# A short convolution moved from 64x64 to 32x32 tiles of the array, in a fused attention and gated-unit kernel

## The chip, the cores and the metric

The kernel runs on one core of one Trainium2 chip. Its time is the device time of one execution in microseconds (us). TensorE multiplies matrices, VectorE (DVE) and ScalarE (ACT) read its results in PSUM and work on them, GpSimd (POOL) converts types and writes masks in SBUF, SyncE (SP) issues nearly all DMAs. Lower is better.

## The reference

The first part is attention over 8 batches of 8 heads, 576 positions and 64 features, causal by blocks of 64 positions. Its output, with the 512 features of a position side by side, is the input `x` of a gated unit:

```python
for k in range(K):                                   # K = 5 taps
    gate_pre += conv_w[k][None, None, :] * xp[:, k:k + S, :]
gate = 1.0 / (1.0 + np.exp(-gate_pre))
val = x @ w_val
return (gate * val @ w_out).astype(np.float32)
```

The convolution works on each feature by itself: five taps along the sequence, padded with four zeros ahead of it. The kernel computes in fp16 with fp32 sums.

## The kernel before

**Attention by pairs of heads.** The loop runs over steps `p`; step p handles one of 32 pairs of heads (four pairs are a batch). The order of the work is written out by hand, and every engine takes its instructions in that order. In the middle of the program one step issues on TensorE, in this order: two score tiles of pair p (`s_tile(p, 0)` and `s_tile(p, 1)`), the product of probabilities and values of pair p-1 (`av`, 30 matmuls in two groups, one for each head), the transposes of q and k of pair p+2 (`trans`, and once a batch `trans_tails`), the third score tile (`s_tile(p, 2)`), one unit of the convolution (`conv`), once a batch `s_last`, the transposes of the finished attention (`xtrans`), one tile of the output projection (`out_tile`), and one chunk of the value projection (`val`).

**Who reads what.** ACT applies exp to each score tile (128x1024 elements) and tanh to the convolution, since a sigmoid is (1 + tanh(z/2))/2, and copies the output tiles. DVE normalises the attention (`rc`, then `x`, for each head), copies the transposed q and k (`qkT`) and x (`xt`), and multiplies gate and value (`gv`). POOL casts q, k and v to fp16 and zeroes the masked probabilities.

**PSUM.** Score tiles have a pool of their own with two buffers of two banks each (`psS`). Everything else takes one of four banks in turn (`gbank`, the tiles G): `av` takes two, `trans`, `trans_tails`, `xtrans` and `out_tile` one each, `conv` two, `val` two. So whoever takes a bank waits until the reader of the bank's last content, four takings earlier, has finished.

**The convolution as matmuls.** Features lie on the partitions in four chunks g of 128. A tap is a matmul with a diagonal block of weights (`DG`) against x shifted by the tap, and five taps add up in PSUM. A 64x64 block uses a quarter of the array, so four such matmuls with different quarters are in work at once: a unit `conv(b, c2, hf)` is half the chunks and half a batch (288 positions), 5 x 4 = 20 matmuls. It puts the features into PSUM in another order, and the columns of `w_val` and the rows of `w_out` are permuted to match when they are loaded and cast (`load_w_out`, `weights`).

**Lags and the end.** Convolution runs at step p for unit p-3, `val` for chunk p-4 of both halves of a batch, and a pair of batches gives nine output tiles. After the last pair of heads, five more steps finish what lags. SP issues the loads of step p (`loads(p)`: q and k of pair p+4, v of pair p+2, weights in the first steps), and after the first output tile its stores stand in the same queue.

Of the kernel before, what the change touches and what calls it, by code (L numbers as in the profile page):

```python
# [10 lines left out]
def kernel(  # L11
# [10 lines left out]
    nc = tc.nc  # L22
# [27 lines left out]
    idfold = const([128, 1, 64], fp16, "idfold")  # L50
# [6 lines left out]
    DG = const([128, 20, 64], fp16, "DG")  # L57

    NV, NPT, NX = 4, 3, 3
    v16s = [const([128, 4, 2, 65], fp16, f"v16_{i}") for i in range(NV)]  # L60
# [10 lines left out]
    def gbank():  # L71
        ring[0] += 1
        return GT[(ring[0] - 1) % 4]
# [171 lines left out]

    th = {}

    def conv(b, c2, hf):
        t = th.get((b, c2))
        if t is None:  # L250
            t = th[(b, c2)] = p3.tile([128, 2, 2, 288], fp32, tag="th", name="th")
        rr = (gbank(), gbank())
        for kk in range(5):
            for row, col in ((0, 0), (1, 1), (0, 1), (1, 0)):
                g = 2 * c2 + col
                rs, cs = slice(64 * row, 64 * row + 64), slice(64 * col, 64 * col + 64)
                mm(rr[row][cs, 0:288], DG[rs, 5 * g + kk, 0:64],
                   xts[b % NX][rs, g, kk + 288 * hf:kk + 288 * hf + 288],
                   start=(kk == 0), stop=(kk == 4))
        for row in range(2):  # L260
            nc.scalar.activation(out=t[0:128, row, hf, 0:288], in_=rr[row][0:128, 0:288],  # L261
                                 func=AF.Tanh, bias=0.0, scale=0.5)

    def val(b, x):
        c2, row = divmod(x, 2)
# [3 lines left out]
        t = th[(b, c2)]  # L269
        for hf in range(2):  # L270
            r = gbank()
            for fc in range(4):
                mm(r[0:128, 0:288], w_val_sb[0:128, fc, 128 * x:128 * x + 128],
                   xts[b % NX][0:128, fc, 4 + 288 * hf:4 + 288 * hf + 288],
                   start=(fc == 0), stop=(fc == 3))
            nc.vector.scalar_tensor_tensor(  # L276
                out=gv[u][0:128, x, bi, hf, 0:288], in0=t[0:128, row, hf, 0:288], scalar=1.0,
                in1=r[0:128, 0:288], op0=ALU.add, op1=ALU.mult)
        if row == 1:
            th.pop((b, c2))  # L280

    def out_tile(u, t):
        g = gv[u][0:128].rearrange("p g b f s -> p g (b f s)")
        r = gbank()
        for fc in range(4):
            mm(r[0:128, 0:512], g[:, fc, 128 * t:128 * t + 128],
               w_out_sb[0:128, fc, 0:512], start=(fc == 0), stop=(fc == 3))
        o = p4.tile([128, 512], fp32, tag="osb", name="osb")
        if u == B // 2 - 1 and t >= 4 and t % 2 == 0:
            nc.vector.tensor_copy(out=o[0:128], in_=r[0:128, 0:512])  # L290
# [16 lines left out]
    for hh in range(2):  # L307
        hs = slice(64 * hh, 64 * hh + 64)
        nc.vector.tensor_copy(out=idfold[hs, 0, 0:64], in_=ident16[hs, 64 * hh:64 * hh + 64])
    load_qk1(1)  # L310
    load_v1(0)
    load_vtail(0)
# [43 lines left out]
        nc.sync.dma_start(out=w_st[0:128, 2 * f:2 * f + 2],  # L356
                          in_=moe_w_val[256 * f:256 * f + 256].rearrange("(f p) n -> p f n", p=128))

    def load_w_out(col):
        for x in range(2):  # L360
            nc.sync.dma_start(
                out=w_st2[64 * col:64 * col + 64].rearrange("p (a x) n -> p a x n", a=2)[:, :, x],
                in_=moe_w_out.rearrange("(a c x i) n -> c x i a n", a=2, c=2, x=2)[col, x])

    def weights(s):
        if s == 1:
            nc.vector.tensor_tensor(out=DG[0:128], in0=idfold[0:128].to_broadcast([128, 20, 64]),
                                    in1=convT[0:128].to_broadcast([128, 20, 64]), op=ALU.mult)
        if 3 < s < 8:
            x = s - 4  # L370
            nc.vector.tensor_scalar(
                out=w_val_sb[0:128, 0:4, 128 * x:128 * x + 128].rearrange(
                    "p f (c i) -> p f c i", c=2),
                in0=w_st[0:128].rearrange("p f (a c r i) -> p f a r c i",
                                          a=2, c=2, r=2)[:, :, x // 2, x % 2],
                scalar1=0.5, scalar2=None, op0=ALU.mult)
        if s in (7, 8):
            a = 2 * (s - 7)
# [19 lines left out]
    for p in range(NP + 5):  # L398
        if p < NP:
            loads(p)  # L400
            if p > 0:
                s_tile(p, 0)
                s_tile(p, 1)
        weights(p)
        if 0 <= p - 1 < NP:
# [5 lines left out]
        if 0 < p < NP:  # L411
# [19 lines left out]
        if 0 <= p - 1 < NP:  # L431
            xtrans(p - 1)

        if p >= 8 and p % 4 == 0:
            b = p // 4 - 2
            outs += [(b // 2, t) for t in (range(4) if b % 2 == 0 else range(4, 9))]
        n = 2 if len(outs) == 5 or p == NP + 4 else 1
        for _ in range(n):
            if outs:
                out_tile(*outs.pop(0))  # L440
        if 0 <= p - 4 < NP:
            val(*divmod(p - 4, 4))
    while outs:
        out_tile(*outs.pop(0))


# [28 lines left out]
```

## Time and profile before

| | |
|---|---|
| time, median of 3 runs | 211.24 us (210.98 to 214.17) |
| the profiled execution's own time | 210.69 us |
| its span, first to last instruction | 208.6 us |
| TensorE busy | 191.0 us, 92% |
| DVE, ACT, POOL busy | 131.0, 140.0, 82.9 us |
| moved by DMA | 40.34 MB, 193 GB/s on the mean |
| mean granted TensorE clock | 0.983 |

In rows of the timeline the first number is the start in us from the beginning of the span, the second the duration, then the engine, the line of the kernel, the operation, the tiles (out<-in), the shape, and xN for N instructions merged; in brackets stands how long the engine sat idle and what ended that. In the chain of waits (the work that ended last, followed back) a row is start, duration and what held the end at that time. In grouped rows the numbers behind the bar are busy us, mean ns of one, and idle us before. A matmul's modelled end includes its way through the array, so the distance between starts is what a stream of them costs.

### The profile page before, as it was taken

To read this page: it belongs to the slowest core of one execution; us is meant where nothing else is said; L and a number is where in the kernel's file an instruction comes from. 1 tells how busy PE (TensorE), PEld (TensorE's weight loads), DVE (VectorE), ACT (ScalarE), POOL (GpSimd) and SP (SyncE) were. 2 spreads that over 40 slices of the span, in tenths; PEclk is the share of its full clock that TensorE was granted. 3 is DMA by queue.
4 is the path that set the end of the run, shared out by engine and by line. 5 is a ranking of instruction groups with operands and counts; after the bars stand their busy time and mean duration, and the time that the engine had idled before them with its cause. 6 is when DMAs were issued, how large, how long until landed. Compare 5 with 4: busy or idle time off the path is not lost.

```text
span 208.6 us, 7431 instructions
## 1 busy us (share of the span) xinstructions
PE 191.0 (92%) x3041; PEld 130.5 (63%) x3041; DVE 131.0 (63%) x282; ACT 140.0 (67%) x205; POOL 82.9 (40%) x168
## 2 busy tenths in 40 slices
PE   4699889988999999999999999999999999999992
PEld 1377656665666766676666766676666766666550
DVE  3349878876667657666667657666667657555351
ACT  4347877657776877668776877668776877783421
POOL 6364654566454441445454441445454441120000
PEclk9958999999999999999999999999999999999999
DMA  5999999999777687765776688665866635111235
GB/s 155 271 262 300 300 262 239 214 208 235 177 199 189 192 236 227 220 186 147 229 206 186 197 231 260 189 184 151 241 197 181 201 101 154 53 50 55 101 141 215
DMA packets 70220, 40.34 MB, mean 193 GB/s; under 512 B 48165, under 2 KB 64549, under 8 KB 70186
## 3 DMA queue, kind: packets, MB, share of 16 engines
q1 hardware_dynamic: 69904, 39.60, 70.6%
q8 instruction: 24, 0.39, 0.8%
q10 hardware_dynamic: 282, 0.27, 0.4%
q14 instruction: 10, 0.08, 0.2%
HBM read 30.42 MB, written 9.44 MB: 191 GB/s over the span
## 4 chain that ended last, share of the span: by engine, by line
PE 53%; DVE 19%; DMA 16%; SPq 6%; issue 3%; POOL 2%; DVEq 0%; POOLq 0%
PE G L33 41%; DVE qkT L162 9%; PE S L33 8%; DVE x L232 6%; DMA vs<-in_v_dram 4%; DMA w_st<-in_moe_w_out_dram 4%; DVE rc L231 3%; SPq L83 3%; DMA tlst<-in_k_dram 3%; PE G L241 3%; DMA vtst<-in_v_dram 3%; SPq L103 2%; DMA qks<-in_k_dram 2%; PE G L151 1%; POOL qk L126 1%
## 5 line engine op out<-in xcount | busy, mean ns | idle before, releaser
L185 ACT ACTIVATE pt<-S 128x1024 f16<-128x1024 f32 x96 | 94.3, 1023 | 32.4 <-PE S L33 31.0
L276 DVE SCALAR_TENSOR_TENSOR gv<-th,G 128x288 f16<-128x288 f32 x64 | 29.1, 455 | 37.1 <-PE G L33 34.8
L201 POOL MEMSET pt<- 64x384 f16 x32 | 13.2, 413 | 93.8 <-ACT pt L185 93.8
L162 DVE COPY qkT<-G 128x1024 f16<-128x1024 f16 x31 | 37.7, 1217 | 2.9 <-PE G L151 2.7
L33 PE MATMUL G<-w_out,gv 128*128 128x512 f16 x144 | 35.8, 378 | 2.5 <-DVE qkT L162 2.5
L33 PE MATMUL G<-xt,w_val 128*128 128x288 f16 x256 | 36.8, 286 | 0.4 <-DVE qkT L162 0.3
L33 PEld LDWEIGHTS <-pt 128*128 128x128 f16 x960 | 31.5, 98 | 7.0 <-issue 6.1
L33 PE MATMUL G<-v,pt 128*128 128x65 f16 x896 | 34.3, 195 | 0.1
L126 POOL CAST qk<-qks 128x1024 f16<-128x1024 f32 x31 | 32.6, 1053 | 4.3 <-DMA qks<-in_k_dram 3.6
L232 DVE TENSOR_TENSOR x<-G,rc 128x320 f16<-128x320 f32 x64 | 31.5, 492 | 2.3 <-DVE rc L231 0.2
L292 ACT COPY osb<-G 128x512 f32<-128x512 f32 x33 | 19.3, 586 | 20.1 <-PE G L33 17.9
L33 PEld LDWEIGHTS <-w_val 128*128 128x128 f16 x256 | 25.0, 98 | 12.1 <-issue 0.7
L33 PE MATMUL S<-qkT 64*128 64x512 f16 (+1 forms) x248 | 28.2, 305 | 0.4 <-ACT pt L195 0.4
L33 PE MATMUL G<-xt,DG 64*64 64x288 f16 x640 | 26.3, 287 | 0.0
L261 ACT ACTIVATE th<-G 128x288 f32<-128x288 f32 x64 | 22.7, 412 | 4.8 <-PE G L33 4.8
L33 PEld LDWEIGHTS <-qkT 64*128 64x128 f16 x496 | 15.1, 95 | 14.6 <-issue 7.3
L33 PEld LDWEIGHTS <-gv 128*128 128x128 f16 x144 | 13.7, 97 | 15.1 <-issue 4.2
L151 PE MATMUL G<-ident,qk 128*128 128x128 f16 x256 | 20.6, 225 | 2.8 <-POOL qk L126 2.7
L231 DVE RECIPROCAL rc<-G 128x5 f32<-128x5 f32 x64 | 12.1, 189 | 15.5 <-PE G L33 15.4
L131 POOL CAST v<-vs 128x512 f16<-128x512 f32 x32 | 20.1, 627 | 3.5 <-PE S L33 1.5
L151 PEld LDWEIGHTS <-qk 128*128 128x128 f16 x256 | 15.6, 101 | 4.1 <-POOL qk L126 3.4
L33 PEld LDWEIGHTS <-DG 64*64 64x64 f16 x640 | 16.2, 105 | 2.7 <-issue 0.5
(51 smaller groups left out, 122.5 us busy)
## 6 DMA issues: line engine op xcount, KB each, us to landing
out_dram<-osb SPq DMA_DIRECT2D x36, 256.0 KB, 2.1
qks<-in_q_dram SPq DMA_DIRECT2D x32, 256.0 KB, 3.7
vs<-in_v_dram SPq DMA_DIRECT2D x64, 128.0 KB, 4.3
qks<-in_k_dram SPq DMA_DIRECT2D x31, 256.0 KB, 3.9
tlst<-in_q_dram SPq DMA_DIRECT2D x8, 128.0 KB, 4.2
tlst<-in_k_dram SPq DMA_DIRECT2D x8, 128.0 KB, 4.2
vtst<-in_v_dram SPq DMA_DIRECT2D x8, 128.0 KB, 4.9
w_st<-in_moe_w_val_dram SPq DMA_DIRECT2D x2, 512.0 KB, 6.1
```

What stands on the lines that cost most here:

```text
L33: nc.tensor.matmul(out=out, lhsT=lhsT, rhs=rhs, start=start, stop=stop, skip_group_check=True)
L126: nc.gpsimd.tensor_copy(out=o, in_=s)
L131: nc.gpsimd.tensor_copy(out=v16s[p % NV][0:128, 0:4, 0:2, 0:64], in_=s)
L151: nc.tensor.transpose(out=r[:, o:o + 128], in_=t[0:128, c, 2 * i:2 * i + 2, 0:64], identity=ident16[0:128, 0:128])
L162: nc.vector.tensor_copy(out=o[0:128].rearrange("p i (s n) -> p i s n", n=4), in_=src)
L185: nc.scalar.activation(out=pts[p % NPT][0:128, 0:2, 512 * t:512 * t + 512], in_=s[0:128, 0:2, 0:512], func=AF.Exp, bias=0.0, scale=0.125)
L201: nc.gpsimd.memset(pt[64:128, 0:2, 0:1536].rearrange("p h (t s) -> p h t s", t=3)[:, :, :, 0:64], 0.0)
L231: nc.vector.reciprocal(out=rc[0:128], in_=O[:, :, 64:65])
L232: nc.vector.tensor_tensor(out=x[0:128, 0:5, h, 0:64], in0=O[:, :, 0:64], in1=rc[0:128].to_broadcast([128, 5, 64]), op=ALU.mult)
L261: nc.scalar.activation(out=t[0:128, row, hf, 0:288], in_=rr[row][0:128, 0:288], func=AF.Tanh, bias=0.0, scale=0.5)
L276: nc.vector.scalar_tensor_tensor(out=gv[u][0:128, x, bi, hf, 0:288], in0=t[0:128, row, hf, 0:288], scalar=1.0, in1=r[0:128, 0:288], op0=AL ...
L292: nc.scalar.copy(out=o[0:128], in_=r[0:128, 0:512])
```

## The change

The convolution's blocks become 32x32, sixteen of them in work at once. A unit is now `conv(b, hf)`: all four chunks of half a batch, 5 x 16 = 80 matmuls of the same 288 columns. Row strip `row` of every chunk goes to a bank of its own; two of the four banks come from the score pool `psS`, two from `gbank`. ACT applies tanh to the two score banks in one instruction and to the other two in one each.

A unit runs every other step (odd p, from 5 on), and `val(b, hf, x)` handles one half batch and one chunk, two a step. Output tiles are freed by half batches (`complete`), and the first comes at step 7 where it came at step 8. The loop ends with the last pair of heads; what remains is written out behind it. The permutation of the weights is by 32 features; `w_out` is loaded in steps 3 and 4 (four DMAs to 32 partitions) where it was in steps 4 and 5 (four to 64 partitions), and cast at steps 6 and 7 where it was at 7 and 8.

```diff
-    def conv(b, c2, hf):
...
-        rr = (gbank(), gbank())
-        for kk in range(5):
-            for row, col in ((0, 0), (1, 1), (0, 1), (1, 0)):
-                g = 2 * c2 + col
-                rs, cs = slice(64 * row, 64 * row + 64), slice(64 * col, 64 * col + 64)
-                mm(rr[row][cs, 0:288], DG[rs, 5 * g + kk, 0:64],
...
+    def conv(b, hf):
+        t = th[(b, hf)] = p2.tile([128, 4, 288], fp32, tag="th", name="th")
+        s = psS.tile([128, 2, 512], fp32, tag="S", name="S")
+        ga, gb = gbank(), gbank()
+        rr = (s[0:128, 0], s[0:128, 1], ga[0:128], gb[0:128])
         for kk in range(5):
+            for d in range(4):
+                for row in range(4):
+                    g = (row + d) % 4
+                    rs, cs = slice(32 * row, 32 * row + 32), slice(32 * g, 32 * g + 32)
+                    mm(rr[row][cs, 0:288], DG[rs, 5 * g + kk, 0:32],
+                       xts[b % NX][rs, g, kk + 288 * hf:kk + 288 * hf + 288],
+                       start=(kk == 0), stop=(kk == 4))
+        nc.scalar.activation(out=t[0:128, 0:2, 0:288], in_=s[0:128, 0:2, 0:288],
+                             func=AF.Tanh, bias=0.0, scale=0.5)
+        for row in (2, 3):
+            nc.scalar.activation(out=t[0:128, row, 0:288], in_=rr[row][:, 0:288],
                                  func=AF.Tanh, bias=0.0, scale=0.5)
...
-        if u == B // 2 - 1 and t >= 4 and t % 2 == 0:
+        if u == B // 2 - 1 and t >= 6 and t % 2 == 0:
             nc.vector.tensor_copy(out=o[0:128], in_=r[0:128, 0:512])
...
-    def load_w_out(col):
...
+    def load_w_out(j):
+        nc.sync.dma_start(
+            out=w_st2[32 * j:32 * j + 32],
+            in_=moe_w_out[128 * j:128 * j + 128].rearrange("(x a) n -> a x n", x=4))
...
-        if p in (4, 5):
-            load_w_out(p - 4)
+        if p in (3, 4):
+            load_w_out(2 * p - 6)
+            load_w_out(2 * p - 5)
...
+    def complete(b, hf):
+        n = 2 * (b % 2) + hf
+        outs.extend((b // 2, t) for t in range(2 * n, 9 if n == 3 else 2 * n + 2))
...
-        if 0 <= p - 3 < NP:
-            bq, un = divmod(p - 3, 4)
-            conv(bq, un // 2, un % 2)
+        bq, m = divmod(p - 5, 4)
+        if bq >= 0 and m % 2 == 0:
+            conv(bq, m // 2)
         if p % 4 == 3 and p + 1 < NP:
             s_last((p + 1) // 4)
...
+        out()
+        if len(outs) > 2:
+            out()
+        if bq >= 0:
+            for x in (0, 1):
+                val(bq, m // 2, 2 * (m % 2) + x)
+            if m % 2 == 1:
+                complete(bq, m // 2)
...
+    b = B - 1
+    av(NP - 1)
+    out()
+    for x in (2, 3):
+        val(b - 1, 1, x)
+    complete(b - 1, 1)
+    xtrans(NP - 1)
+    out()
+    conv(b, 0)
+    out()
+    conv(b, 1)
+    out()
+    for hf in range(2):
+        for x in range(4):
+            val(b, hf, x)
+            out()
+        complete(b, hf)
     while outs:
-        out_tile(*outs.pop(0))
+        out()
```

First place: TensorE in one step in the middle of the program, before the change. One matmul of each group is shown; S_ are score tiles, G0 to G3 the four banks, ident16 marks a transpose.

```order
L33 MATMUL G3_106<-v16t_0_89,pt4_0_96 128x65
...
L151 MATMUL G0_103<-ident16_76,qk16_2217 128x128
...
L33 MATMUL S_2327<-kt_0_98,qkT_2060 128x64
...
L33 MATMUL G1_104<-xt_0_100,DG_84 64x288
...
L241 MATMUL G3_106<-ident16_76,x16_2280 128x128
...
L33 MATMUL G0_103<-w_out_79,gv_1729 128x512
...
L33 MATMUL G1_104<-xt_0_100,w_val_78 128x288
...
L33 MATMUL G2_105<-xt_0_100,w_val_78 128x288
```

The same engine with the change, in step 20, one of the steps that have no convolution.

```order
L33 MATMUL G2_105<-v16t_1_90,pt4_1_97 128x65
...
L151 MATMUL G3_106<-ident16_76,qk16_2225 128x128
...
L33 MATMUL S_2411<-kt_0_98,qkT_2099 128x64
...
L241 MATMUL G0_103<-ident16_76,x16_2364 128x128
...
L33 MATMUL G1_104<-w_out_79,gv_2026 128x512
...
L33 MATMUL G2_105<-xt_2_102,w_val_78 128x288
...
L33 MATMUL G3_106<-xt_2_102,w_val_78 128x288
```

Before, the output tile takes the bank that the transposes of q and k used in the same step (G0); now it takes the first bank of `av` (G1), and the second chunk of `val` takes the transposes' bank (G3).

Second place: ACT over one step with the convolution and `s_last`, before. pt is exp's output, th tanh's, osb an output tile.

```order
L185 ACTIVATE pt_0_93<-S_2062 128x2x512
L261 ACTIVATE th_2080<-G3_106 128x288
L261 ACTIVATE th_2080<-G0_103 128x288
L195 ACTIVATE pt4_0_96<-S_2103 128x512
L292 COPY osb_2123<-G2_105 128x512
```

With the change, step 19:

```order
L185 ACTIVATE pt_0_93<-S_2209 128x2x512
L261 ACTIVATE th_2227<-S_2228 128x576
L264 ACTIVATE th_2227<-G3_106 128x288
L264 ACTIVATE th_2227<-G0_103 128x288
L195 ACTIVATE pt4_0_96<-S_2312 128x512
L291 COPY osb_2332<-G2_105 128x512
```

The convolution's score buffer S_2228 comes between S_2209 (the third score tile) and S_2312 (`s_last`), so with two buffers `s_last` now writes the one that exp of the third score tile reads; before, S_2103 had the other.

Third place: SP's queue around the loads of `w_out`, before.

```order
L103 DMA vs_456<-in_v_dram 128x4x64 x2
L92 DMA tlst<-in_q_dram 64x8x64
L92 DMA tlst<-in_k_dram 64x8x64
L83 DMA qks_576<-in_q_dram 128x2x256
L83 DMA qks_576<-in_k_dram 128x2x256
L103 DMA vs_579<-in_v_dram 128x4x64 x2
L361 DMA w_st_81<-in_moe_w_out_dram 64x2x512 x2
L83 DMA qks_698<-in_q_dram 128x2x256
L83 DMA qks_698<-in_k_dram 128x2x256
L103 DMA vs_701<-in_v_dram 128x4x64 x2
L361 DMA w_st_81<-in_moe_w_out_dram 64x2x512 x2
```

With the change:

```order
L103 DMA vs_458<-in_v_dram 128x4x64 x2
L359 DMA w_st_81<-in_moe_w_out_dram 32x4x512 x2
L92 DMA tlst<-in_q_dram 64x8x64
L92 DMA tlst<-in_k_dram 64x8x64
L83 DMA qks_557<-in_q_dram 128x2x256
L83 DMA qks_557<-in_k_dram 128x2x256
L103 DMA vs_560<-in_v_dram 128x4x64 x2
L359 DMA w_st_81<-in_moe_w_out_dram 32x4x512 x2
L83 DMA qks_646<-in_q_dram 128x2x256
L83 DMA qks_646<-in_k_dram 128x2x256
L103 DMA vs_649<-in_v_dram 128x4x64 x2
```

Each pair of `w_out` loads now stands ahead of the q, k and v of one more step: v of pair 6 (vs_579 before, vs_560 now) comes behind one pair of them where it came behind none, and v of pair 7 behind both where it came behind one.

More of the change, by code (lines that the diff above doesn't have):

```diff
@@ L56 @@
     convT = const([128, 20, 1], fp16, "convT")
[L57 removed]
+    DG = const([128, 20, 32], fp16, "DG")
     NV, NPT, NX = 4, 3, 3
@@ L246, with val @@
     th = {}
[L248 to L261 removed]
+    def conv(b, hf):
[3 more added lines that the diff above has]
+        rr = (s[0:128, 0], s[0:128, 1], ga[0:128], gb[0:128])
+        for kk in range(5):
+            for d in range(4):
[9 more added lines that the diff above has]
+            nc.scalar.activation(out=t[0:128, row, 0:288], in_=rr[row][:, 0:288],
                                  func=AF.Tanh, bias=0.0, scale=0.5)
[L264 to L265 removed]
+    def val(b, hf, x):
         u, bi = divmod(b, 2)
@@ L268, in val @@
             gv[u] = p2.tile([128, 4, 2, 2, 288], fp16, tag="gv", name="gv")
[L269 to L280, printed above, removed]
+        t = th[(b, hf)]
+        r = gbank()
+        for fc in range(4):
+            mm(r[0:128, 0:288], w_val_sb[0:128, fc, 128 * x:128 * x + 128],
+               xts[b % NX][0:128, fc, 4 + 288 * hf:4 + 288 * hf + 288],
+               start=(fc == 0), stop=(fc == 3))
+        nc.vector.scalar_tensor_tensor(
+            out=gv[u][0:128, x, bi, hf, 0:288], in0=t[0:128, x, 0:288], scalar=1.0,
+            in1=r[0:128, 0:288], op0=ALU.add, op1=ALU.mult)
     def out_tile(u, t):
@@ L306 @@
         nc.vector.memset(ktails[i][0:128, 0:4, 1:2, 64:128], 0.0)
-    for hh in range(2):
-        hs = slice(64 * hh, 64 * hh + 64)
-        nc.vector.tensor_copy(out=idfold[hs, 0, 0:64], in_=ident16[hs, 64 * hh:64 * hh + 64])
+    for i in range(4):
+        hs = slice(32 * i, 32 * i + 32)
+        nc.vector.tensor_copy(out=idfold[hs, 0, 0:32], in_=ident16[hs, 32 * i:32 * i + 32])
     load_qk1(1)
@@ L393, in loads, with out @@
             load_w_val(p - 1)
-        if p in (4, 5):
-            load_w_out(p - 4)
+        if p in (3, 4):
+            load_w_out(2 * p - 6)
+            load_w_out(2 * p - 5)
     outs = []
[L398 to L403, printed above, removed]
+    def complete(b, hf):
+        n = 2 * (b % 2) + hf
+        outs.extend((b // 2, t) for t in range(2 * n, 9 if n == 3 else 2 * n + 2))
+    def out():
+        if outs:
+            out_tile(*outs.pop(0))
+    for p in range(NP):
+        loads(p)
+        if p > 0:
+            s_tile(p, 0)
+            s_tile(p, 1)
         weights(p)
-        if 0 <= p - 1 < NP:
+        if p > 0:
             av(p - 1)
@@ L410 @@
                 trans_tails((p + 2) // 4)
-        if 0 < p < NP:
+        if p > 0:
             s_tile(p, 2)
```

33 lines of the change are left out of this document (9 added, 24 removed).

## The prediction

> **What bounds the kernel now.** I read the page, then the chain of waits, then the timeline of one step. The page's busy times and its chain by engine:
>
> ```profile
> PE 191.0 (92%) x3041; PEld 130.5 (63%) x3041; DVE 131.0 (63%) x282; ACT 140.0 (67%) x205; POOL 82.9 (40%) x168
> PE 53%; DVE 19%; DMA 16%; SPq 6%; issue 3%; POOL 2%; DVEq 0%; POOLq 0%
> ```
>
> TensorE is busy 92%, yet only 53% of the chain: a fifth goes through DVE. Where, the chain shows for step 17, the pattern of the whole middle:
>
> ```profile
> 100.38 2.00 PE G L33 x12
> 102.38 0.54 PE S L33 x6
> 102.92 0.57 PE G L33 x15
> 103.75 0.26 DVE x L232
> 104.37 0.49 DVE x L232
> 104.86 1.14 DVE qkT L162
> ```
>
> From the first head's product the end is held by DVE: normalise twice, then copy qkT until 106.0. TensorE's timeline, steps 17 to 19:
>
> ```profile
> 102.31 0.61 PE L33 MATMUL S<-qkT 64*128 64x512 f16 x6
> 102.85 0.60 PE L33 MATMUL G<-v,pt 128*128 128x65 f16 x14
> 103.32 0.59 PE L33 MATMUL G<-v,pt 128*128 128x65 f16 x14
> 103.77 0.61 PE L151 MATMUL G<-ident,qk 128*128 128x128 f16 x8
> 104.32 0.28 PE L33 MATMUL S<-qkT 64*128 64x256 f16 x2
> 104.65 0.81 PE L33 MATMUL G<-xt,DG 64*64 64x288 f16 x20
> 105.39 0.45 PE L241 MATMUL G<-ident,x 128*128 128x128 f16 x5
> 106.05 1.02 PE L33 MATMUL G<-w_out,gv 128*128 128x512 f16 x4 [0.20 <-DVE qkT L162]
> 106.91 1.14 PE L33 MATMUL G<-xt,w_val 128*128 128x288 f16 x8
> 107.98 0.61 PE L33 MATMUL S<-qkT 64*128 64x512 f16 x6
> 111.72 0.44 PE L241 MATMUL G<-ident,x 128*128 128x128 f16 x5 [0.33 <-DVE qkT L162]
> 112.05 1.02 PE L33 MATMUL G<-w_out,gv 128*128 128x512 f16 x4
> ```
>
> A step is 5.67 us (102.31 to 107.98). The convolution costs TensorE 0.74 of it (104.65 to 105.39) and the output tile then still waits for qkT, whose bank it takes. So 0.74 us of TensorE is not 0.74 us of the step: what counts is who waits for qkT.
>
> **The change: the convolution itself.** It goes from 32 units of 0.74 us to 16 units of 80 matmuls. Inside a unit now:
>
> ```profile
> 104.65:104.66 0.01, 0.01 (x4) 0.01 (x4) 0.00 (x0) 1.00 0.41 146
> 104.66:104.80 0.13, 0.13 (x4) 0.13 (x8) 0.00 (x0) 1.00 0.67 85
> L33 PEld LDWEIGHTS <-DG 64*64 64x64 f16 x640 | 16.2, 105 | 2.7 <-issue 0.5
> ```
>
> (Busy time and counts of TensorE and its weight loads on DG alone, in windows of 14 and 133 ns; then the group of those loads.) Four matmuls and their four loads start within 14 ns, 3.5 ns a pair, and then nothing but the next loads starts until the 288 columns are through. A group costs its columns, not its pairs. If that holds for sixteen, a unit costs 0.74 + 12 x 0.0035 = 0.78 us, my value: 12.5 us in all where it is 23.7.
>
> The other end is that pairs come one behind the other as in `av`: 15 of them from 102.85 to 103.32, 31 ns each, 80 x 0.031 = 2.48 us. Nowhere in the trace would more than four matmuls fit the array at once, so it cannot decide; I take the windows, as the row of the same operation. The Trainium skill's page "TensorE: Matmul & The Clock Gate" (Back-to-back issue gap) says that warm matmuls never start closer than about 25 ns however small; by it a unit would be 2.0 us. The trace disagrees between different quarters of the array (3.5 ns), and agrees within one (31 ns for 65 columns).
>
> **The steps.** ACT and DVE in step 17, and ACT's prices:
>
> ```profile
> 102.80 3.04 ACT L185 ACTIVATE pt<-S 128x1024 f16<-128x1024 f32 x3 [0.78 <-PE S L33]
> 103.52 0.20 DVE L231 RECIPROCAL rc<-G 128x5 f32<-128x5 f32 x1 [0.58 <-PE G L33]
> 104.78 1.22 DVE L162 COPY qkT<-G 128x1024 f16<-128x1024 f16 x1
> L185 ACT ACTIVATE pt<-S 128x1024 f16<-128x1024 f32 x96 | 94.3, 1023 | 32.4 <-PE S L33 31.0
> L195 ACT ACTIVATE pt<-S 128x512 f16<-128x512 f32 x8 | 4.9, 612 | 2.0 <-PE S L33 2.0
> L261 ACT ACTIVATE th<-G 128x288 f32<-128x288 f32 x64 | 22.7, 412 | 4.8 <-PE G L33 4.8
> ```
>
> I count from a step's first score matmul; an output tile is 0.86 (106.05 to 106.91), `val` 1.07 (to 107.98). Third score tile done 2.34, second normalisation 2.55 (104.86), qkT 3.70 (106.0), second exp 2.5 and third exp 3.53 (102.80 + 3.04). The joint tanh of 576 elements lies between 512 (612 ns) and 1024 (1023): 0.66 us.
>
> - p mod 4 = 1, convolution: its score buffer is free after the second exp, so it runs 2.5 to 3.28, xtrans follows, and the output tile waits for qkT until 3.74 as now. The gate's tanh (third exp 3.53 + 0.66 + 0.36) ends at 4.55, just ahead of `val` at 4.60. Step 5.67, nothing gained.
> - mod 4 = 0, none: xtrans waits for the second normalisation until 2.60, takes 0.33 (111.72 to 112.05), the output tile has av's bank and starts at 2.93, `val` at 3.79; its second chunk waits for qkT, long done. 2.93 + 0.86 + 1.07 = 4.86.
> - mod 4 = 2, none, with the tails' transposes: xtrans at 2.65 no longer waits for qkT as at 111.72; 4.91.
> - mod 4 = 3: `s_last` now needs the buffer that the third exp reads, so it waits until 3.55; 0.22 for it, 0.33, 0.86, 1.07: 6.03. xtrans, the output tile and `val` are queued behind it.
>
> POOL has to keep up with the short steps:
>
> ```profile
> 96.71 0.54 PE S L33 x6
> 101.46 1.05 POOL L126 CAST qk<-qks 128x1024 f16<-128x1024 f32 x1
> ```
>
> The cast of q and k ends 5.80 after step 16's first score matmul, and the transposes ask for it 1.46 into the next step, so after a step of 4.86 with 0.5 us to spare. SP's loads of a step are issued behind the output tile's store, which moves with the step.
>
> Steps 9 to 30 are 6, 5, 6 and 5 of the kinds 1, 0, 2, 3: 34.0 + 24.3 + 29.5 + 30.2 = 117.9, and two second output tiles of 0.86, 119.7 us. Before:
>
> ```profile
> 55.34 0.61 PE L33 MATMUL S<-qkT 64*128 64x512 f16 x6
> 183.79 0.61 PE L33 MATMUL S<-qkT 64*128 64x512 f16 x6
> 204.74 0.69 DVE osb L290
> ```
>
> 128.45 us from step 9 to step 31, three second tiles in it. Gain 8.8 us.
>
> **The start.** Until then DMA leads:
>
> ```profile
> 21.00:31.00 10.00, 8.54 (x187) 6.36 (x184) 8.07 (x18) 7.80 (x11) 5.84 (x11) 1.00 1.07 278
> 33.50:46.00 12.50, 11.05 (x215) 8.35 (x214) 10.91 (x25) 8.98 (x12) 5.85 (x11) 1.00 1.14 213
> 37.25 8.41 DMA w_st<-in_moe_w_out_dram
> 43.80 0.87 POOL L131 CAST v<-vs 128x512 f16<-128x512 f32 x1 [1.49 <-PE S L33]
> 45.72 0.62 PE L151 MATMUL G<-ident,qk 128*128 128x128 f16 x8 [0.85 <-POOL qk L126]
> 51.47 0.62 PE L151 MATMUL G<-ident,qk 128*128 128x128 f16 x8 [0.91 <-POOL qk L126]
> ```
>
> (DMA's share and GB/s end the first two rows.) With `w_out` in the queue the rate falls from 278 to 213 GB/s. POOL's cast of v of pair 7 at 43.80 waits for its load (the score tile named was long done), q and k of pair 9 are cast behind it, and the transposes wait for those. One more pair of `w_out` loads, 0.52 MB at 213 GB/s, comes ahead: 2.5 us. So these transposes go from 45.72 to 48.2; step 7 then ends by the walk above (third tile from 48.8, its exp done 50.25, `s_last`, xtrans, output, `val`) at 52.8, and step 8 at 57.6, against 55.34: 2.3 us lost. The convolution and `val` that steps 3 and 4 no longer run hide in the same waits. Bounds: no delay, if the loads overlap (-0.2 us), and 3.1 us, if a pair costs its bytes at 278 (1.9 us) and half of what the slow stretch lost (12.5 - 12.5 x 213/278 = 2.9).
>
> **The end.** From step 31 on there are, in `av`s, score tiles, units, xtrans, `val`s of 0.535 and output tiles: before 1.84 + 0.87 + 4 x 0.74 + 0.6 + 10 x 0.535 + 10 x 0.86; now two more `val`s and one convolution less at 0.78 each, +0.5 us. Waits to add: the convolution for the second exp (0.6), `val` behind its tanh (0.15), the last convolution's bank for the tanh before it (0.25), the last three output tiles for the last gv (0.5). 2.0 us later; the last copy and store are as now.
>
> Sum: -8.8 + 2.3 + 2.0 = -4.5 us. The span goes from 208.6 to 204.1, the profiled execution's 210.69 to **206.2 us**. The runs' median was 211.24, 0.55 above that execution. Code ahead of step 2 (smaller DG, two more copies) and the two DVE casts in step 6 lie under these loads; if not, the copies cost 0.4 us at rc's 0.20.
>
> **Rivals.**
> - *Pairs come one by one.* Slower. A longer unit c is free up to 0.91 us in kind 1 (3.74 - 2.5 - 0.33) and 1.05 in kind 3, and costs fully at the end and in the first two: 6(c - 0.91) + 5(c - 1.05) + 5(c - 0.78) = 16c - 14.6. The gain is gone at c = 1.19 us, 15 ns a pair. At 31 ns, c = 2.48: +25 us, 231 us. For it: 80 matmuls in 0.6 us is denser than anything in the trace. Against: the 3.5 ns. The 25 ns rule named above would give 2.0 us, +17 us, 224.
> - *The next group's weights are not loaded ahead,* since sixteen matmuls stand in between, not four. Four loads of 105 ns are exposed: c = 1.20, +4.6 us, 210.8. No change. Against it: four loads start beside four running matmuls in the second window.
> - *The loads of `w_out` cost nothing there:* 2.5 us less, 203.7. For it: the wait is DMA's total, which is the same by step 8.
>
> **Chances.** My forecast 0.45 (204 to 208.5), pairs one by one 0.17, weights late 0.18, `w_out` free 0.14, else 0.06. The measurement tells 2%, 4.2 us, from no change: below 207.0 lie 0.31 of the forecast and the 0.14, together 0.45; within, 0.34; above 215.5, 0.21. The range goes from 201.5 (`w_out` free, and `s_last` without its 5 waits of 0.4) to 214 (c = 1.4); it leaves out nearly all of the slow case.
>
> **What would show it.** A group of DG matmuls at 0.78 us a unit, starts of sixteen within some 60 ns. Steps alternating between 4.9 and 5.7 to 6.0 us; the wait for qkT gone from the output tile in even steps; `s_last` waiting for ACT. The first score matmul of step 9 near 57.6, of step 31 near 177. Wrong it is if a unit takes over 1.2 us, or even steps stay above 5.3.

## The result and the profile after

| | before | after |
|---|---|---|
| time, median of 4 runs each, one comparison | 212.13 us (210.98 to 214.17) | 205.77 us (205.13 to 206.10) |
| ratio | | 0.971, 95% interval 0.964 to 0.978 |
| the profiled execution's own time, and its span | 210.69 and 208.6 us | 205.13 and 203.2 us |
| first score matmul of step 9, of step 31 | 55.34, 183.79 us | 57.83, 177.31 us |
| steps 9 to 31, and from there to the end of the span | 128.45, 24.8 us | 119.48, 25.9 us |

The change makes the kernel 2.9% faster. A second comparison of the same two kernels gave 206.92 us and 0.977 (0.974 to 0.981). The ratios leave out single executions that took over 1.5% longer than the fastest of their kernel (the longest, of a cause that no run shows, 332 us for the changed kernel and 912 us for `s_last` a step later, there the profiled one). In the profiled executions the loop gains 8.97 us, the start loses 2.49 and the end 1.1.

The page of the changed kernel, its busy times and its chain by engine, then by line:

```profile
PE 183.9 (91%) x3681; PEld 128.5 (63%) x3681; DVE 129.1 (64%) x283; ACT 140.1 (69%) x190; POOL 82.0 (40%) x168
PE 59%; ACT 14%; DMA 11%; issue 7%; DVE 5%; POOL 2%; SPq 0%; ACTq 0%; POOLq 0%; DVEq 0%
PE G L33 39%; ACT pt L185 14%; PE S L33 11%; DMA qks<-in_k_dram 8%; PE G L241 5%; DMA vs<-in_v_dram 3%; PE G L151 3%; DVE x L232 3%; DVE rc L231 1%; POOL qk L126 1%; PE G L138 1%; DVE idfold L308 1%; DVE qk L157 0%; DVE osb L289 0%; DVE ident L303 0%
```

TensorE is busy 7 us less. DVE's part of the chain falls from 19% to 5%, and `qkT` has left the list: it held the end in the middle steps before. ACT's exp takes 14%. The chain through steps 16 and 17 shows the two kinds of step:

```profile
97.90 0.50 DVE x L232
...
98.45 0.45 PE G L241 x5
98.90 1.84 PE G L33 x12
...
102.09 1.03 ACT pt L185
...
103.16 0.29 PE S L33 x2
```

Step 16 has no convolution, and its xtrans (line 241) follows the second normalisation (line 232) directly. In step 17 the convolution waits for the second exp, since it writes to the score buffer which that exp reads. TensorE's timeline of steps 17 and 18; of the 80 matmuls of the unit the first rows of the five taps are shown:

```profile
100.68 0.61 PE L33 MATMUL S<-qkT 64*128 64x512 f16 x6
...
103.16 0.29 PE L33 MATMUL S<-xt,DG 32*32 32x288 f16 x2
...
103.28 0.30 PE L33 MATMUL S<-xt,DG 32*32 32x288 f16 x2
...
103.46 0.30 PE L33 MATMUL S<-xt,DG 32*32 32x288 f16 x2
...
103.61 0.30 PE L33 MATMUL S<-xt,DG 32*32 32x288 f16 x2
...
103.77 0.30 PE L33 MATMUL S<-xt,DG 32*32 32x288 f16 x2
...
104.14 0.45 PE L241 MATMUL G<-ident,x 128*128 128x128 f16 x5
104.43 1.03 PE L33 MATMUL G<-w_out,gv 128*128 128x512 f16 x4
105.29 1.14 PE L33 MATMUL G<-xt,w_val 128*128 128x288 f16 x8
106.36 0.61 PE L33 MATMUL S<-qkT 64*128 64x512 f16 x6
...
108.97 0.45 PE L241 MATMUL G<-ident,x 128*128 128x128 f16 x5
109.26 1.03 PE L33 MATMUL G<-w_out,gv 128*128 128x512 f16 x4
110.13 1.14 PE L33 MATMUL G<-xt,w_val 128*128 128x288 f16 x8
111.20 0.61 PE L33 MATMUL S<-qkT 64*128 64x512 f16 x6
```

Step 17 lasts 5.69 us (100.68 to 106.36) and step 18 4.84 (to 111.20). The unit takes 0.98 us from its first matmul to xtrans (103.16 to 104.14), not 0.78. Its first sixteen matmuls start within 54 ns, as foreseen, and the next sixteen within 66 ns. From the third tap on they come mostly at 8.3 ns a pair of matmul and weight load within a tap. The waits of TensorE in the middle of the program (60 to 170 us) come to one row (engine and line, what was waited for, us in total, times, longest); first those of the kernel before:

```profile
PE G L33 <- DVE qkT L162: 1.8, 8, 0.3
PE G L241 <- DVE qkT L162: 1.6, 5, 0.3
```

and all that the same view has of the changed kernel:

```profile
PE G L241 <- DVE x L232: 0.8, 4, 0.2
```

The waits for qkT are gone. The points by which the start can be judged, from the timelines of POOL and TensorE after:

```profile
46.76 0.62 POOL L131 CAST v<-vs 128x512 f16<-128x512 f32 x1
48.41 0.62 PE L151 MATMUL G<-ident,qk 128*128 128x128 f16 x8 [0.59 <-POOL qk L126]
52.99 0.61 PE L33 MATMUL S<-qkT 64*128 64x512 f16 x6
57.83 0.61 PE L33 MATMUL S<-qkT 64*128 64x512 f16 x6
```

### The profile page after: what moved, and what is told of

It reads as the page before. It is cut to its first block, busy times and chain, and to the rows that moved or that the text cites. A ratio compares the mean times of both kernels' runs of the same rounds, so it can differ in the third digit from the quotient of the medians.

```text
span 203.2 us, 8654 instructions
## 1 busy us (share of the span) xinstructions
PE 183.9 (91%) x3681; PEld 128.5 (63%) x3681; DVE 129.1 (64%) x283; ACT 140.1 (69%) x190; POOL 82.0 (40%) x168
## 4 chain that ended last, share of the span: by engine, by line
PE 59%; ACT 14%; DMA 11%; issue 7%; DVE 5%; POOL 2%; SPq 0%; ACTq 0%; POOLq 0%; DVEq 0%
PE G L33 39%; ACT pt L185 14%; PE S L33 11%; DMA qks<-in_k_dram 8%; PE G L241 5%; DMA vs<-in_v_dram 3%; PE G L151 3%; DVE x L232 3%; DVE rc L231 1%; POOL qk L126 1%; PE G L138 1%; DVE idfold L308 1%; DVE qk L157 0%; DVE osb L289 0%; DVE ident L303 0%
## 5 line engine op out<-in xcount | busy, mean ns | idle before, releaser
L277 DVE SCALAR_TENSOR_TENSOR gv<-th,G 128x288 f16<-128x288 f32 x64 | 28.4, 454 | 26.1 <-PE G L33 24.8
L33 PEld LDWEIGHTS <-pt 128*128 128x128 f16 x960 | 32.5, 100 | 7.3 <-issue 3.8
L33 PE MATMUL G<-w_out,gv 128*128 128x512 f16 x144 | 36.5, 379 | 0.0
L33 PE MATMUL G<-v,pt 128*128 128x65 f16 x896 | 35.4, 197 | 0.2
L291 ACT COPY osb<-G 128x512 f32<-128x512 f32 x34 | 20.0, 589 | 14.4 <-PE G L33 13.2
L151 PE MATMUL G<-ident,qk 128*128 128x128 f16 x256 | 21.3, 231 | 5.3 <-POOL qk L126 5.3
L243 DVE COPY xt<-G 128x576 f16<-128x576 f16 x32 | 14.5, 452 | 8.9 <-PE G L241 8.9
L33 PEld LDWEIGHTS <-gv 128*128 128x128 f16 x144 | 12.7, 98 | 10.1 <-DVE gv L277 0.5
L33 PE MATMUL S<-xt,DG 32*32 32x288 f16 x640 | 17.0, 295 | 1.3 <-ACT pt L185 0.5
L33 PE MATMUL G<-xt,DG 32*32 32x288 f16 x640 | 17.1, 296 | 0.0
```

The source lines that it names most:

```text
L33: nc.tensor.matmul(out=out, lhsT=lhsT, rhs=rhs, start=start, stop=stop, skip_group_check=True)
L151: nc.tensor.transpose(out=r[:, o:o + 128], in_=t[0:128, c, 2 * i:2 * i + 2, 0:64], identity=ident16[0:128, 0:128])
L243: nc.vector.tensor_copy(out=xts[b % NX][0:128, g, 4:4 + SEQ], in_=r[:, 0:SEQ])
L277: nc.vector.scalar_tensor_tensor(out=gv[u][0:128, x, bi, hf, 0:288], in0=t[0:128, x, 0:288], scalar=1.0, in1=r[0:128, 0:288], op0=ALU.add, ...
```

## The experiments

All times are medians, and each ratio is to the kernel before in the same comparison. Step lengths are distances between the first score matmuls of following steps, by p mod 4, where no second output tile stands in the step:

| us | mod 1 | mod 2 | mod 3 | mod 0 | steps 9 to 31 |
|---|---|---|---|---|---|
| before | 5.67 | 6.00 | 5.67 | 5.67 | 128.45 |
| after | 5.69 | 4.84 | 6.04 | 4.84 | 119.48 |
| the new order with 64x64 tiles | 6.06 | 4.84 | 6.29 | 4.84 | 122.91 |
| after, `s_last` a step later | 5.68 | 4.84 | 5.69 | 4.93 | 118.39 |
| after, with the old turn of the banks | 5.69 | 6.01 | 6.04 | 5.67 | 129.42 |
| before, its unit in the score banks | 5.45 | 5.53 | 6.04 | 5.45 | 125.84 |

**The narrow tiles alone.** The new order stays, with the same units of half a batch, but the blocks are 64x64 again, four at once, 40 matmuls a unit. The permutations of the weights and their loads go with it.

```diff
-            for d in range(4):
-                for row in range(4):
-                    g = (row + d) % 4
-                    rs, cs = slice(32 * row, 32 * row + 32), slice(32 * g, 32 * g + 32)
-                    mm(rr[row][cs, 0:288], DG[rs, 5 * g + kk, 0:32],
+            for c2 in range(2):
+                for row, col in ((0, 0), (1, 1), (0, 1), (1, 0)):
+                    g = 2 * c2 + col
+                    rs, cs = slice(64 * row, 64 * row + 64), slice(64 * col, 64 * col + 64)
+                    mm(rr[2 * c2 + row][cs, 0:288], DG[rs, 5 * g + kk, 0:64],
```

> The changed program with its new order, banks and half batches, but each unit's convolution in 64x64 tiles (40 matmuls, four in work at once, in the same four banks). Theory (the gain is TensorE's time for the convolution, priced by the walk through a step): a unit takes 2 x 0.74 = 1.48 us; odd steps grow from 5.69 to about 6.2 (p mod 4 = 1) and from 6.04 to about 6.5 (mod 4 = 3), even steps stay at 4.84, the end is 1.5 us longer: about 213 us, no gain against before. Rival (the gain comes from the new order and the rotation of the banks): about 206 us, as the changed kernel.

207.8 us in 4 runs, ratio 0.973 (0.966 to 0.980). The unit, in TensorE's timeline (the first two of its ten groups of four matmuls, and what follows the last):

```profile
104.74 0.32 PE L33 MATMUL S<-xt,DG 64*64 64x288 f16 x4
104.86 0.32 PE L33 MATMUL G<-xt,DG 64*64 64x288 f16 x4
...
106.09 0.45 PE L241 MATMUL G<-ident,x 128*128 128x128 f16 x5
```

A group every 0.12 us, and 1.35 us for the unit, not 1.48: twice the old unit's groups, but its way out of the array only once. The odd steps are longer than after's by 0.37 and 0.25 us, as a unit longer by 0.375 would have it that is partly covered (in steps mod 4 = 3 by 0.13 us that `s_last` waits in the changed kernel); the even ones are the same. The loop is 3.43 us longer than after's and the end 1.0 (26.9). The time, 207.8, lay between what the two theories had, and nearer to the one for which the tiles' width matters less.

**The same two kernels side by side**, the change itself and the wide tiles again, in one comparison with more runs:

> The changed kernel itself once more, as the measure for the others of this series. 205.8 us; the first score matmul of step 9 between 56 and 59 us, since executions of one kernel differ there.

> The kernel with the new order and 64x64 tiles again, timed beside the changed kernel. Its loop from step 9 to 31 took 122.9 us against 119.5 in the profiles, and its end 1.0 us more. Theory (the narrow tiles are worth those 4.4 us, the rest of the gain is the order): 4 to 4.5 us above the changed kernel of this series, about 210. Rival (the start gives part of it back): 1.5 to 2 us above it, as the first timing had it.

The change 206.92 us (0.977, 0.974 to 0.981), wide tiles 210.42 us (0.9945, 0.991 to 0.998): 3.5 us between them, where the two profiles give 4.4 for loop and end. The loop of the wide tiles is 122.93 us, as at first; so the difference to the first comparison (0.973) arose outside the loop, and it shows how much the start of this kernel differs between executions and comparisons. What follows: half as many units in the new order shorten the loop by 5.5 us, but in this comparison start and end take nearly all of it back, and the narrow tiles make a difference of 2% out of it. In the first comparison the two kernels could not be told apart by their ratios (0.973 and 0.971); the 3.43 us of the loop and the 1.0 of the end stand in the profiles of both.

**What limits a unit.** Taps 1 to 4 work on 64 of the 288 columns, which leaves out these taps for the other 224; the number of the instructions and their order are the same.

```diff
+                    n = 288 if kk == 0 else 64
-                       xts[b % NX][rs, g, kk + 288 * hf:kk + 288 * hf + 288],
+                       xts[b % NX][rs, g, kk + 288 * hf:kk + 288 * hf + n],
```

> The changed kernel with the taps 1 to 4 of the convolution on 64 of the 288 columns only (the other columns get tap 0 alone), so that the array's own time of a group is 27 ns and what feeds it shows. Theory (a queue of some 64 instructions is full when a unit starts, behind it 4.17 ns an instruction, 8.3 ns a pair): 32 pairs within about 0.12 us and then 8.3 ns a pair, last start about 0.52 us into a unit. Rival 1 (sixteen tiles take a group's columns and 3.4 ns a pair, and the spread in the changed kernel's later groups is memory contention): 3.4 ns a pair throughout, last start about 0.35 us. Rival 2 (25 ns a matmul): about 2.0 us. The time falls by 1 us at most in any of the first two.

206.6 us in its one run, and the loop is 119.42 us, as after. First row of each tap, and the last:

```profile
105.02 0.29 PE L33 MATMUL S<-xt,DG 32*32 32x288 f16 x2
...
105.14 0.20 PE L33 MATMUL S<-xt,DG 32*32 32x64 f16 x2
...
105.33 0.20 PE L33 MATMUL S<-xt,DG 32*32 32x64 f16 x2
...
105.47 0.21 PE L33 MATMUL S<-xt,DG 32*32 32x64 f16 x2
...
105.60 0.20 PE L33 MATMUL S<-xt,DG 32*32 32x64 f16 x2
...
105.72 0.20 PE L33 MATMUL G<-xt,DG 32*32 32x64 f16 x2
105.86 0.45 PE L241 MATMUL G<-ident,x 128*128 128x128 f16 x5
```

With less than a quarter of the columns the third and fourth tap start where they did: 0.31 and 0.45 us after the first, where after has 0.30 and 0.45. From the third tap on 16 pairs take 0.13 to 0.14 us, 8.3 ns a pair, whatever their columns. The 288 columns show only later: the fifth tap starts at 0.58 us where after has 0.61, the last matmul at 0.71 where after has 0.76, and the unit takes 0.83 us instead of 0.98. So in the third and fourth tap it is not the array that a unit waits for; instructions come at 8.3 ns a pair once the first 32 pairs, which went at 3.6 and 4.4 ns (54 and 66 ns a tap), are used up. The theory had this rate right and the last start wrong, 0.52 us. Why there are 32, and why the third tap starts 0.19 us behind the second where 16 pairs take 0.13, this run doesn't tell.

**The turn of the banks.** In steps without a convolution two banks of the ring are passed over, so that the output tile and xtrans take the banks they took before. Nothing else changes.

```diff
         if bq >= 0 and m % 2 == 0:
             conv(bq, m // 2)
+        elif bq >= 0:
+            ring[0] += 2
```

> The changed kernel with two of the four banks skipped in every step without a convolution, so that the output tile (mod 4 = 0) or xtrans (mod 4 = 2) takes the bank of the transposes of q and k again, as before the change. The work and its order are the same. Theory (even steps are short because nothing early waits for qkT): steps mod 4 = 0 go from 4.84 to 5.67 and mod 4 = 2 from 4.84 to 6.0, about 11 us more, 217 us, all gain lost though the convolution is as short as before. Rival (even steps are short because the convolution is missing in them): they stay below 5.2, under 209 us.

217.31 us, ratio 1.028 (1.024 to 1.033). TensorE's timeline in step 16 of this kernel, one without convolution, and behind it DVE's copy of qkT in the same step:

```profile
101.55 0.61 PE L33 MATMUL S<-qkT 64*128 64x512 f16 x6
...
104.16 0.45 PE L241 MATMUL G<-ident,x 128*128 128x128 f16 x5 [0.20 <-DVE x L232]
105.28 1.02 PE L33 MATMUL G<-w_out,gv 128*128 128x512 f16 x4 [0.67 <-DVE qkT L162]
...
107.22 0.61 PE L33 MATMUL S<-qkT 64*128 64x512 f16 x6
```

```profile
104.02 1.21 DVE L162 COPY qkT<-G 128x1024 f16<-128x1024 f16 x1
```

Half the units are gone, and the step is 5.67 us as before: TensorE waits 0.67 us for qkT where it used to run the convolution. Steps mod 4 = 2 are 6.01 us, there with up to 1.2 us of xtrans waiting for qkT. This is the clearest of the runs: the loop is 9.9 us longer than after's, and only the turn of the banks differs. Against the kernel before, the loop is only 1.0 us longer; the rest of the loss is the later start (step 9 at 60.40 us) and the longer end. The convolution's TensorE time had lain in front of a wait, and taking it away is worth nothing until the wait goes as well; it went only because a step without a convolution takes two banks fewer from the ring.

**The banks alone.** The kernel before, in its own order with 32 units, but each unit's two banks come from the score pool instead of the ring.

```diff
-        rr = (gbank(), gbank())
+        s = psS.tile([128, 2, 512], fp32, tag="S", name="S")
+        rr = (s[0:128, 0], s[0:128, 1])
```

> The kernel before the change with one edit: a unit's two banks come from the score pool, so that the banks G go round in seven takings a step and the output tile takes av's. Nothing of the tiles, the units or the lags is changed. By the walk through a step: steps mod 4 = 1, 0 are 5.53 (TensorE's own sum, the convolution starting at 2.5), mod 4 = 2 5.6 where it was 6.0, mod 4 = 3 6.03 where it was 5.67, since s_last then waits for the third exp: 127.2 us from step 9 to 31 against 128.4, so about 1 us gained. Theory (the bank frees the end of a step, but the time must also be taken from TensorE): that. Rival (the wait for qkT alone is the gain): 5 us or more.

209.87 us, ratio 0.990 (0.985 to 0.995). The loop is 2.6 us shorter, which is 1.4 more than I expected. Its waits of TensorE in the middle:

```profile
PE S L33 <- ACT pt L185: 1.5, 5, 0.3
```

qkT is gone from that list here too, and what comes instead is `s_last`, which now waits for the third exp in steps mod 4 = 3 (6.04 us where it was 5.67). So leaving the ring is good for a quarter to a third of the loop's gain by itself (2.6 of 8.97 us). The wide tiles' run, with half as many units, had 5.5, and the narrow tiles added the last 3.4; how the parts divide depends on the order in which they are added. The whole time gains 0.5 to 1.5%.

**`s_last` a step later**, where no convolution holds a score buffer:

```diff
-        if p % 4 == 3 and p + 1 < NP:
-            s_last((p + 1) // 4)
+        if p % 4 == 0 and p > 0:
+            s_last(p // 4)
```

> The changed kernel with s_last of a batch moved from the step mod 4 = 3, where it stands behind the convolution, to the next step, where there is none. Theory (s_last waits for the buffer that the third exp reads): steps mod 4 = 3 go from 6.04 to 5.69, steps mod 4 = 0 from 4.84 to about 4.97, in all 1.2 to 1.6 us less, about 204.4 us. Rival (those steps end on ACT's or DVE's chain anyway): both kinds together stay at 10.9 us a pair, 205.8.

> The changed kernel with s_last in the steps mod 4 = 0, for the lengths of its steps: mod 4 = 3 from 6.04 to 5.69, mod 4 = 0 from 4.84 to 4.97; about 204.4 us.

204.43 us, 0.959 (0.953 to 0.965), and in the repeat 204.55 us, 0.966 (0.957 to 0.974). The steps are read in the repeat; TensorE in its steps 19 (mod 3) and 20:

```profile
113.31 0.61 PE L33 MATMUL S<-qkT 64*128 64x512 f16 x6
...
116.77 0.45 PE L241 MATMUL G<-ident,x 128*128 128x128 f16 x5
...
119.00 0.61 PE L33 MATMUL S<-qkT 64*128 64x512 f16 x6
...
121.76 0.29 PE L33 MATMUL S<-kt 64*128 64x64 f16 x8 [0.35 <-ACT pt L185]
```

Steps mod 4 = 3 go from 6.04 to 5.69 us (113.31 to 119.00): the 0.35 us that this kind had over kind 1 are gone. Not all of it was waiting. In the chain of the changed kernel, step 19:

```profile
113.71 1.03 ACT pt L185
114.79 0.29 PE S L33 x8
```

`s_last` starts there when the third exp ends, 1.10 us behind the unit's first matmul, where xtrans starts 0.98 behind it in the other kind: 0.13 us of wait, and 0.22 of its own until xtrans at 115.01. In its new place `s_last` costs 0.09 us a step; only in step 20 does it wait for ACT by 0.35 us, and that step is 5.21. The loop is 1.1 us shorter. The intervals of the ratios overlap with those of the changed kernel (0.971 and 0.977), so what this is worth is read from the loop.

**The loads of `w_out`**, in steps 4 and 5 as in the kernel before, both casts at step 7:

```diff
-        if s in (6, 7):
-            a = 2 * (s - 6)
+        for a in ((0, 2) if s == 7 else ()):
...
-        if p in (3, 4):
-            load_w_out(2 * p - 6)
-            load_w_out(2 * p - 5)
+        if p in (4, 5):
+            load_w_out(2 * p - 8)
+            load_w_out(2 * p - 7)
```

> The changed kernel with the loads of w_out in steps 4 and 5 as before the change, and both casts of them in step 7. Theory (one pair of these loads ahead of v of pair 7 costs 2.5 us of DMA time that nothing gives back): the first score matmul of step 9 goes from 57.8 to about 55.5, total about 203.5 us. Rival (DMA has the same bytes to move by step 8 either way): step 9 stays within 0.5 us of 57.8, total about 205.7.

> The kernel with the loads of w_out in steps 4 and 5 again, for its interval. Against the changed kernel's ratios of 0.971 and 0.977: theory (one pair of loads out of the way of v of pair 7 is worth 2 us), ratio 0.963; rival (the start's luck), 0.972.

203.93 us, 0.957 (0.950 to 0.963), and 204.23 us, 0.968 (0.964 to 0.973). The mean spans are 202.1 and 202.0 us, against 203.8 and 204.6 for the changed kernel's two sets of runs: about 2 us, near the 2.3 of the theory. The ratio of the repeat, 0.968, lies between what theory and rival had (0.963 and 0.972); by the intervals it is apart from 0.977 and not from 0.971, so the gain is likely, but not firm. The profiled executions don't show it: step 9 starts at 58.22 and 58.98, not earlier than after's 57.83. In both, TensorE stood still inside the unit of step 7, with nothing waited for; the chain of the repeat:

```profile
47.61 1.63 issue
49.23 0.30 PE G L33 x2
```

**No `w_out` at all.** The loads are left out and the weights set to zero, which leaves out the true output projection, but not its work on TensorE; a memset stands where POOL's casts stood.

```diff
-            nc.gpsimd.tensor_copy(out=w_out_sb[0:128, a:a + 2, 0:512],
-                                  in_=w_st2[0:128, a:a + 2, 0:512])
+            nc.gpsimd.memset(w_out_sb[0:128, a:a + 2, 0:512], 0.0)
```

> The changed kernel without the loads of w_out (left out: its weights are set to zero, by a memset where the cast stood), everything else as it is. Theory (the start is DMA's, and these 1.05 MB cost it about 2.5 us a half megabyte): the first score matmul of step 9, 57.8 to 59.7 in the executions so far, comes 4 to 5 us earlier, total about 201.5 us. Rival (what holds steps 5 to 8 is the loads of q, k and v and POOL's casts of them, whatever the weights do): less than 1.5 us.

201.21 us (201.03 to 201.51), 0.954 (0.951 to 0.957). In TensorE's timeline, steps 8 and 9:

```profile
49.35 0.61 PE L33 MATMUL S<-qkT 64*128 64x512 f16 x6
...
54.19 0.61 PE L33 MATMUL S<-qkT 64*128 64x512 f16 x6
```

Both start 3.6 us earlier than after's (52.99 and 57.83), and the loop that follows is the same, 119.38 us. The mean span is 199.4 us, 4.4 below after's. So about 4 us of the changed kernel are its `w_out` loads, all of them ahead of step 9, and the start is DMA's. From 30 to 43 us the two profiles have 245 GB/s without these loads and 192 with them, at a DMA share of 1.09 and 1.18, so the loads bring a low rate with them besides their bytes. Without them the runs also differ by 0.5 us where the other kernels' differ by 1 to 4.

**Both moves together** (`s_last` and the loads):

> The changed kernel with s_last in the steps mod 4 = 0 and the loads of w_out in steps 4 and 5. If the two are independent, 1.4 and 1.7 us less: 202.6 us, with pairs of steps of 10.67 instead of 10.88 us and step 9 earlier by 1.5 us. If s_last's earlier time was the start's luck, 204.

203.67 us (202.47 to 206.02), 0.961 (0.957 to 0.965), beside 206.92 for the change in the same comparison. This is the lowest median of the complete kernels, and by its ratio it is faster than both kernels that the document compares; but it is not below either move by itself (ratios of 0.957 to 0.968). The 1.1 us of the loop are there (118.41 us), and the earlier step 9 is not in the profiled execution (59.59 us), so the 202.6 us of two independent gains was missed.

## Why the prediction was right

The forecast of 206.2 us met 205.77, and 205.13 for the profiled execution, for which it was worked out and in which its steps can be followed one by one. The waits and the four kinds of step were right; two terms, the unit and the end, were not.

- **qkT's wait is the bound.** Right, and it is what the whole gain hangs on: with the old turn of the banks the loop is 129.42 us where before has 128.45, with the convolution as short as it is.
- **The four kinds of step**, forecast at 5.67, 4.86, 4.91 and 6.03 us, measured 5.69, 4.84, 4.84 and 6.04. The joint sum of the loop, 119.7, measured 119.48. The tails' step (mod 4 = 2) was put 0.07 too high.
- **The unit, 0.78 us.** This term was mis-sized: it is 0.98. The 3.5 ns a pair, read in groups of four, holds for sixteen different tiles at once (54 ns), but only for two taps; then a feed of 8.3 ns a pair decides. The rivals by which pairs come at 25 or 31 ns are refuted. The Trainium skill's floor of about 25 ns ("TensorE: Matmul & The Clock Gate", Back-to-back issue gap), which the prediction weighed, does not hold between tiles. The Trainium skill has, on the same page, "TensorE: Matmul & The Clock Gate", in other sections (The mechanism, and Measured speedup vs the span model), about 4 ns between the starts on different tiles; with that the trace agrees for the first two taps (3.6 and 4.4 ns), not for the others (8.3). The rival "weights late" had 1.20 us, about as far above the measured 0.98 as the forecast lay below, and its reason is refuted: loads of the next sixteen weights run while sixteen matmuls are in work, and the second tap starts 0.12 us behind the first, as the groups of the wide tiles do.
- **Why the wrong unit cost next to nothing in the loop.** The prediction's slack, 0.91 us in kind 1 and 1.05 in kind 3, nearly covered it: kind 1 became longer by 0.02 us and kind 3 by 0.01. In kind 1 the unit is 0.07 over the slack, but xtrans took 0.29 us, not 0.33, and the unit began 0.02 earlier, which is luck. Only the end had to pay for it.
- **The price of a still longer unit** was 16 us for each us, with the gain gone at 1.19. The wide tiles (1.35 us) lengthen loop and end by 4.4 us for 0.375, 12 for each us, and at 1.35 the kernel is still 0.6 us below the one before in the second comparison (in the first, 5). The break-even lies near 1.4 by the second, not at 1.19.
- **`s_last` waits for the third exp.** Right: it starts at the exp's end, and steps mod 4 = 3 are 0.35 us longer than kind 1, 0.13 of it wait and 0.22 its own. The forecast's 0.27 of wait was less because the longer unit stands in the same time.
- **The start, +2.3 us.** 2.49 in the profiled executions, and every point on the way came within 0.5 us: the cast of v at 46.76 (46.3), the transposes 48.41 (48.2), step 8 at 52.99 (52.8), step 9 at 57.83 (57.6). That the four points fit so well is partly luck: step 9 of the same changed kernel began at 59.65 us in its second profile. With loop and end taken as constant, the mean spans give a loss of 3.6 us in the second comparison (208.9 before, 204.6 after) and of 2.0 in the first (about 209.7, the times less 2.1 us, and 203.8). The cause, the loads of `w_out`, is supported by their removal (step 9 at 54.19). That it is their earlier place is likely, from the 2 us that moving them back gave, but no profile shows step 9 earlier by it. The rival "`w_out` free", with step 9 at 55.1, fits neither profile of the changed kernel.
- **The end, +2.0 us.** Mis-sized: +1.1. This is the term that was furthest off. The last three output tiles were to wait 0.5 us for the last gv, and they run through without a gap, twelve matmuls in a row in TensorE's timeline of the changed kernel:

```profile
196.44 2.90 PE L33 MATMUL G<-w_out,gv 128*128 128x512 f16 x12
```

Of the waits that were added up only the one for the exp is in the waits after 177 us (0.5, priced at 0.6), and a wait of the same size that before had there, for `x`, is gone; the three units, each 0.2 us longer than priced, add 0.6 back. So the two mis-sized terms, the unit and the end's waits, have opposite signs, and that is a part of why the total is so close, which is luck too.

## What to carry to other kernels

Ask of work that is to be made shorter not what it costs on its engine, but what waits behind it: here 0.74 us of convolution stood in front of a wait that took its place when it went, and the steps became shorter by 0.83 us and more only where the convolution and the two banks it took went together (the banks alone gave 0.22 to 0.47 in three of the four kinds, the convolution alone nothing). When a ring of buffers is shared, count takings per step: the change of their number moves who waits for whom, and may be worth more than the work that was saved. And let a longer or shorter variant of the disputed piece have its slack worked out first; a term that lies inside a slack need not be known well.

## What the runs showed of the hardware that was not expected

- Sixteen 32x32 tiles do work at once, at 3.6 ns a matmul with its weight load in the first tap (54 ns) and 4.4 in the second (66 ns), so for 32 pairs; from then on a stream of pairs runs mostly at 8.3 ns each, with 64 columns as with 288. Sixteen tiles of 288 columns need 122 ns a round by the columns (the distance of the first two taps) and 133 by this feed, so shorter rows gain little from the third round on: 0.05 us up to the last start, as the run with 64 columns shows. The Trainium skill ("TensorE: Matmul & The Clock Gate", The mechanism) speaks of a window of 64 instructions through which TensorE takes weight loads ahead; 32 pairs are 64 instructions, but no run here varies the count, so that this is the cause is not shown.
- While the loads fill DMA's time, TensorE can stop for 0.6 to 2.0 us inside a run of matmuls with nothing to wait for (1.63 us in the lines above, 2.01 ahead of `av` and 0.59 in the unit in the first profile with late `w_out`). 16 KB of instructions were fetched by DMA close to that time in the repeat (46.4 us), which fits a late fetch of instructions; such fetches also stand where nothing stops (36.5 us in the profile of the changed kernel), no run tested it, and it stays open.
- The granted TensorE clock fell to half in the start of the changed kernel, behind 4 us (28 to 32) in which TensorE was busy for 2.2, with waits of 1.2 and 0.6 us (windows of 2 us; the last three figures of a row are the granted clock, DMA's share and GB/s):

```profile
30.00:32.00 2.00, 1.18 (x22) 0.95 (x23) 1.93 (x6) 0.71 (x1) 0.18 (x1) 1.00 1.14 172
...
34.00:36.00 2.00, 0.76 (x15) 0.60 (x13) 1.33 (x4) 0.58 (x1) 1.60 (x2) 0.50 1.15 215
36.00:38.00 2.00, 2.00 (x59) 1.55 (x59) 0.95 (x1) 0.34 (x1) 0.00 (x0) 0.50 1.19 241
```

The first unit, at 37.49 us, took 1.40 us in that stretch instead of 0.98. In the profile before, the clock was 1.00 over the whole of 30 to 60 us. In the second profile of the changed kernel the clock was 0.50 from 42 to 48 us, behind 4 us with 0.21 us of TensorE work. Of the 1.82 us by which its step 9 comes later, 0.65 stand ahead of the transposes of step 6 (44.26 us against 43.61) and 1.17 behind them, where the clock was half until 48 us. So a start that waits more for its loads can lose a second time, in the work that follows the wait, and this is likely a part of why starts of one kernel differ; no run varied it by itself.
